# Nine of sixteen x tiles come turned from HBM, and the last products of the second layer come in halves

## The chip, the cores and the metric

The kernel runs on one core of a Trainium2 chip. The core has five engines that run side by side and wait for one another by semaphores: TensorE (PE in the profile; its loads of the stationary operand are PEld), VectorE (DVE), ScalarE (ACT), GpSimd (POOL) and SyncE (SP), which here issues nearly all transfers. The metric is the time of one execution on the device in microseconds, lower is better. The median of three runs before is 492.32 us.

## What is computed

x is 2048 rows of 512 numbers in float32. A layer norm of each row, then two branches on the result, and `x + s * silu(B)` at the end:

```python
xn = (x - mean) / sqrt(var + 1e-5)              # over the 512 columns
q, k, v = split(xn @ wqkv)                      # 32 heads of 16
phi_q = [softmax(q w_phi), softmax(-q w_phi)]   # per head, phi_k alike
s = (phi_q (phi_k^T v)) / (phi_q sum(phi_k) + 1e-6) @ wo
B = mish(xn @ w1 + b1) @ w2                     # 512 -> 1792 -> 512
out = x + s * silu(B)
```

## The kernel before

The 2048 rows are sixteen tiles of 128 rows, t = 0 to 15. Every large product is made of three matmuls: both operands are split into a high part (rounded) and a low part (the rest), and low x high, high x low and high x high are added up in PSUM. ACT makes a high part, DVE or POOL the low part (`split`). The k and v projections, the first layer and one half of the second take seven block products in place of eight, so that sums and differences of two tiles (t and t + 4) are needed as well: `sums_x` makes them (`ts`, split into `th` and `tl`).

`norm(t)` brings a tile to the form in which the products read it, with the 512 columns on the partitions. It loads the tile as x (128 rows on the partitions), takes mean and variance per row on DVE (`bn_stats`, `bn_aggr`), 1/sqrt on POOL (`pow`), normalises the tile on DVE or ACT, turns it with four matmuls against an identity matrix into one PSUM bank `pt`, and splits that bank into the slot `xT`. The bank is read again by `sums_x`, where tile t + 4 is first copied out of PSUM (`xr`), since POOL cannot read there.

Tiles 8 to 15 of the second layer (steps Ga to Gd of the list, `ffn2a` to `ffn2d`) go through the seven products. `ffn2d` is the last: for each of seven blocks b it takes the sum `t4`, split into the slot `md`, and adds its product to the two banks `xb[1][0]` and `xb[1][1]` (x_0 and x_1 below). After the seventh block these banks are the results of output tiles 10 and 11, and `final` (steps E10, E11) applies silu on ACT, multiplies by s and adds x on DVE or POOL, and stores. `PIECES` cuts tile 10 into two and tile 11 into four column pieces there.

Nothing is scheduled by the hardware or by a compiler. The steps in `ORDER` write one long list of operations; `SCHED` is a second list that gives the order in which these are issued, by number, with the engine behind the number where an operation could go to two (V for DVE, G for POOL, A for ACT). `PLACE` gives for each tile the buffer that it lies in. Each engine then takes its own instructions strictly in that order, waiting where an operand or a buffer is not ready. All are issued from one line (L182 before, L185 after), so the profile has to be read by the names of tiles. SP issues the transfers in the same manner; they use eight completion semaphores in turn, so that each transfer also waits for the one eight places ahead of it.

At the start `WAKE` matmuls of ones run on PE while the first loads are on their way, and then eight "folds" (`wkf`, `wqf`: four matmuls each of a weight tile with w_phi).

## Time and profile before

| | before |
|---|---|
| median of three runs | 492.32 us (492.06 to 492.81) |
| profiled execution, its own time | 492.47 us |
| span, first to last instruction | 490.7 us |
| PE busy | 482.5 us, 98% of the span |
| DVE, POOL, ACT busy | 428.0, 276.8, 270.1 us |
| bytes moved | 115.53 MB, 235 GB/s mean |
| granted TensorE clock | 0.996 mean |

A row of a timeline gives the start in us from the span's start, the duration of the group, engine, line, operation, `out<-in`, the size and the count; in square brackets stands how long the engine was idle ahead of it and what ended the wait. A row of the groups view gives `busy us, mean ns of one | idle time before`. A matmul's duration includes its way through the array, and the next one starts before it has ended, so throughput is read from the distance between starts.

### The profile page before, as it was taken

To read this page: it belongs to the slowest core of one execution; us is meant where nothing else is said; L and a number is where in the kernel's file an instruction comes from. 1 tells how busy PE (TensorE), PEld (TensorE's weight loads), DVE (VectorE), ACT (ScalarE), POOL (GpSimd) and SP (SyncE) were. 2 spreads that over 40 slices of the span, in tenths; PEclk is the share of its full clock that TensorE was granted. 3 is DMA by queue.
4 is the path that set the end of the run, shared out by engine and by line. 5 is a ranking of instruction groups with operands and counts; after the bars stand their busy time and mean duration, and the time that the engine had idled before them with its cause. 6 is when DMAs were issued, how large, how long until landed. Compare 5 with 4: busy or idle time off the path is not lost.

```text
span 490.7 us, 8536 instructions
## 1 busy us (share of the span) xinstructions
PE 482.5 (98%) x3126; PEld 397.9 (81%) x3126; DVE 428.0 (87%) x658; ACT 270.1 (55%) x408; POOL 276.8 (56%) x204
## 2 busy tenths in 40 slices
PE   9999999999999999999999999999999999999994
PEld 9888888888888788887888778888888887888883
DVE  5998989999989998989999978979956699889974
ACT  4777754544071524333434778587496487657721
POOL 2889556986548657567575687353642334612440
PEclk9999999999999999999999999999999999999998
DMA  8736838344977689979788896867686652484366
GB/s 296 286 123 243 303 126 338 152 133 120 375 253 265 207 289 342 287 258 298 264 268 286 319 351 233 278 196 234 214 288 230 211 193 67 152 276 154 107 203 203
DMA packets 65592, 115.53 MB, mean 235 GB/s; under 512 B 7056, under 2 KB 32016, under 8 KB 65552
## 3 DMA queue, kind: packets, MB, share of 16 engines
q1 hardware_dynamic: 65408, 114.75, 68.6%
q8 instruction: 24, 0.39, 0.3%
q10 hardware_dynamic: 144, 0.26, 0.1%
q14 instruction: 16, 0.13, 0.1%
HBM read 72.92 MB, written 42.07 MB: 234 GB/s over the span
## 4 chain that ended last, share of the span: by engine, by line
PE 94%; DVE 3%; issue 1%; DMA 1%; POOL 0%; SPq 0%; ACT 0%; DVEq 0%; ACTq 0%
PE y L182 19%; PE fx L182 14%; PE q L182 9%; PE pw L182 9%; PE kx L182 8%; PE fy L182 8%; PE x L182 6%; PE ky L182 4%; PE fz L182 3%; PE pn L182 2%; PE kz L182 2%; PE z L182 2%; PE kvp L182 2%; PE pt L182 1%; PE k L182 1%; PE v L182 1%
## 5 line engine op out<-in xcount | busy, mean ns | idle before, releaser
L182 PE MATMUL q<-wqh,xT 128*128 128x512 f32 x128 | 43.0, 395 | 0.0
L182 ACT ACTIVATE r<-r,b1t 128x512 f32<-128x512 f32 x56 | 37.9, 715 | 3.0 <-DMA r<-hd 3.0
L182 PEld LDWEIGHTS q<-wqh,xT 128*128 128x128 f32 x128 | 24.0, 188 | 5.1
L182 PE MATMUL q<-wql,xT 128*128 128x512 f32 x64 | 25.0, 390 | 0.0
L182 DVE TENSOR_REDUCE tz<-ez 128x64 f32<-128x1024 f32 x16 | 19.3, 1204 | 1.3 <-POOL ez L182 1.3
L182 ACT ACTIVATE hb<-fx 128x512 f32<-128x512 f32 x13 | 7.5, 593 | 18.4 <-PE fx L182 18.4
L182 PE MATMUL kx<-wss,th 128*128 128x512 f32 x56 | 17.3, 390 | 0.0
L182 POOL TENSOR_TENSOR w2t<-w2t 128x256 f32<-128x256 f32 (+1 forms) x4 | 6.0, 1496 | 19.7 <-DVE w2t L182 12.9
L182 ACT ACTIVATE qs<-q 128x512 f32<-128x512 f32 x12 | 6.9, 595 | 17.9 <-PE kvp L182 10.0
L182 POOL TENSOR_TENSOR rs<-rs,mhalf 128x1 f32<-128x1 f32 x16 | 9.8, 620 | 12.0 <-DVE rs L182 11.3
L182 DVE TENSOR_TENSOR ol<-pn,oh 128x256 fp32r<-128x256 f32 x32 | 12.1, 415 | 4.9 <-ACT oh L182 4.9
L182 ACT ACTIVATE hc<-fx 128x512 f32<-128x512 f32 x13 | 7.7, 598 | 15.0 <-PE fx L182 15.0
L182 ACT ACT_TABLE_LOAD x12 | 15.4, 1283 | 0.2
L182 ACT ACTIVATE w1sh<-w1s 128x1024 fp32r<-128x1024 f32 x7 | 7.4, 1059 | 11.8 <-DVE w1s L182 6.2
L182 PEld LDWEIGHTS q<-wql,xT 128*128 128x128 f32 x64 | 12.0, 188 | 2.3
L182 DVE BATCH_NORM_STATS2 st<-x 128x6 f32<-128x512 f32 x16 | 10.7, 682 | 3.6 <-DMA x<-x 3.6
L182 POOL TENSOR_TENSOR w<-w2r,w 128x512 fp32r<-128x512 f32 x7 | 9.0, 1295 | 8.5 <-ACT w L182 8.5
L182 DVE TENSOR_TENSOR xT<-pt,xT 128x512 fp32r<-128x512 f32 x16 | 10.8, 680 | 2.0 <-ACT xT L182 1.2
L182 PE MATMUL pw<-oh,wo0l 128*128 128x512 f32 x32 | 12.5, 390 | 0.0
L182 PE MATMUL pw<-ol,wo0h 128*128 128x512 f32 x32 | 12.5, 389 | 0.0
L182 PE MATMUL pw<-oh,wo0h 128*128 128x512 f32 x32 | 12.5, 389 | 0.0
L182 PE MATMUL pw<-oh,wo1l 128*128 128x512 f32 x32 | 12.4, 389 | 0.0
(862 smaller groups left out, 1864.3 us busy)
## 6 DMA issues: line engine op xcount, KB each, us to landing
r<-hd SPq DMA_DIRECT2D x28, 512.0 KB, 5.3
qd<-qs SPq DMA_DIRECT2D x16, 256.0 KB, 6.3
scr<-xT SPq DMA_DIRECT2D x8, 512.0 KB, 5.3
...
```

What stands on the lines that cost most here:

```text
L182: getattr(g, m)(*a, **k)
```

## The change

Nine tiles (`TURNED`: 3, 6, 7, 9, 10, 11, 13, 14, 15) are no longer turned on PE. The tile is still loaded as x, for the mean and variance. These now stand in the first two columns of a block of 32 columns (`mv`, cleared by POOL first); the reciprocal deviation replaces the variance; DVE turns the block in squares of 32 x 32 (`turn`), so that four of its rows hold the means and four the deviations, 32 numbers or 128 bytes in each. Two transfers write these as two rows of 128 numbers to HBM (`row`), a third reads them back spread over all 128 partitions (`bc`). The tile itself is loaded a second time from `xt`, the transposed copy of x that `final` already uses (`nx`, 512 pieces of 512 bytes). A subtraction and a multiplication of 128 x 512 (DVE or POOL) normalise it, and it lies in SBUF, so that the low part and the sums may go to POOL, and no copy `xr` is needed where tile t + 4 is such a tile.

The last step `ffn2d` becomes three. `ffn2e` splits `t4` (slot `me`) and adds its product to x_0; `ffn2f` and `ffn2g` add to the first and the second half of the columns of x_1, with matmuls of 256 columns. In `ORDER` all of x_0 and its `final` now stand ahead of the second halves.

`WAKE` goes from 13 to 10, and `SCHED` and `PLACE` are new throughout. The first rows of the lists are shown in the diff; what they do is shown by engine below it.

```diff
--- before.py
+++ after.py
@@ -26,9 +26,9 @@
 SLOTS, S2, RQ = 38, 15, 5
-WAKE = 13
+WAKE = 10
 PIECES = {10: 2, 11: 4}
-PLAIN = (0,)
+TURNED = (3, 6, 7, 9, 10, 11, 13, 14, 15)
 GROUPS = ((0, 1, 2, 3), (4, 5, 6))
 ORDER = """
...
-E8 Gc7 O12 Gc8 Gc9 Gc10 Gc11 Gc12 Gc13 Gd7 Gd8 E9 Gd9 Gd10 O10 Gd11 Gd12 E14 E15 E12 E13 Gd13 E10 E11
+E8 Gc7 O12 Gc8 Gc9 Gc10 Gc11 Gc12 Gc13 Ge7 Ge8 E9 Ge9 Ge10 O10 Ge11 Ge12 E14 E15 E12 E13 Ge13 Gf7 Gf8 Gf9 Gf10 Gf11
+Gf12 Gf13 E10 Gg7 Gg8 Gg9 Gg10 Gg11 Gg12 Gg13 E11
 """
 SCHED = """
-27 16 0 13 1 46 2 19 3 15 4 74 5 17 28 6 96 7 14 18 8 123 9 29 10 30 47 20 11 31 12 42 129 48 32 49 33V 50 120 21 51
...
+10 43 0 71 1 12 2 24 238 3 208 93 281 4 13 11 5 14 6 44 15 7 120 45 8 46 72 117 47 9 35 94 48 73 49A 74 25 126 75 36
...
 PLACE = """
-0 2 7 3 1 4 1 6 8 0 3 15 22 2 6 0 0 0 1 7 3 3 9 6 8 4 1 3 1 2 4 10 5 5 13 13 23 30 12 11 14 6 0 5 2 6 7 16 8 4 1 4 7 5
...
+0 0 6 2 17 3 5 7 8 6 12 21 25 3 1 4 5 5 6 9 8 5 10 4 7 1 4 1 3 0 1 18 2 2 11 14 24 30 22 11 15 0 6 2 4 3 4 13 7 7 3 0
...
@@ -324,10 +327,35 @@
         Q.dma_start(xx, x[t * P:(t + 1) * P, :])
         return xx
 
+    def norm_turned(t, mv):
+        rs = mv[:, 1:2]
+        V.tensor_scalar(rs, rs, 1e-5, None, op0=ALU.add)
+        G.tensor_tensor(rs, rs, mhalf, op=ALU.pow)
+        tr = sm([P, 32], f"turn{t}")
+        V.transpose(tr, mv)
+        row = dram.tile([2, P], F32, name=f"row{t}")
+        for c in range(2):
+            Q.dma_start(row[c].rearrange("(b n) -> b n", b=4), tr.rearrange("(b c) n -> c b n", c=32)[c])
+        bc = alloc("s2", [P, 2, P], f"bc{t}")
+        Q.dma_start(bc.rearrange("p c n -> p (c n)"), row.rearrange("c n -> (c n)").partition_broadcast(P))
+        nx = alloc("s2", [P, KC, P], f"nx{t}")
+        Q.dma_start(nx, xt.rearrange("(k p) n -> p k n", p=P)[:, :, t * P:(t + 1) * P])
+        for c, op in ((0, ALU.subtract), (1, ALU.mult)):
+            either(nx, nx, bc[:, None, c, :].to_broadcast([P, KC, P]), op=op)
+        return nx
+
     def norm(t):
         xx = load_x(t)
         st = sm([P, 6], f"st{t}")
         V.bn_stats(st, xx)
+        if t in TURNED:
+            mv = sm([P, 32], f"mv{t}")
+            G.memset(mv, 0.0)
+            V.bn_aggr(mv[:, 0:2], st)
+            w = slot([P, 2, KC, P], f"xT{t}", F32R)
+            pt = norm_turned(t, mv)
+            split(pt, w[:, 0], w[:, 1], either)
+            return keep_x(t, w, pt)
         mv = alloc("st", [P, 2], f"mv{t}")
         V.bn_aggr(mv, st)
         rs = alloc("st", [P, 1], f"rs{t}")
@@ -344,6 +372,9 @@
             for k in range(KC):
                 PE.transpose(pt[:, k, :], xx[:, k * P:(k + 1) * P], ident)
         split(pt, w[:, 0], w[:, 1])
+        keep_x(t, w, pt)
+
+    def keep_x(t, w, pt):
         xT[t], pts[t] = w, pt
         g, i = divmod(t, 4)
         Q.dma_start(scr[g][:, i], f32(w)[:, :, g % 2 * 2:])
@@ -352,18 +383,21 @@
 
     def sums_x(t):
         p1, p2 = pts.pop(t), pts.pop(t + 4)
-        xr = s2(f"xr{t}")
-        copy(xr, p2.rearrange("p k n -> p (k n)"))
-        xr = xr.rearrange("p (k n) -> p k n", k=KC)
+        xr = p2
+        if p2.space == "PSUM":
+            xr = s2(f"xr{t}")
+            copy(xr, p2.rearrange("p k n -> p (k n)"))
+            xr = xr.rearrange("p (k n) -> p k n", k=KC)
+        first = V.tensor_tensor if p1.space == "PSUM" else either
         ts = slot([P, 4, 2, P], f"ts{t}")
-        V.tensor_tensor(ts[:, 0], xr[:, 0:2], p1[:, 0:2], op=ALU.subtract)
+        first(ts[:, 0], xr[:, 0:2], p1[:, 0:2], op=ALU.subtract)
         with one():
             V.tensor_tensor(ts[:, 1], p2[:, 2:4], ts[:, 0], op=ALU.subtract)
             G.tensor_tensor(ts[:, 1], xr[:, 2:4], ts[:, 0], op=ALU.subtract)
         with one():
             V.tensor_tensor(ts[:, 2], p2[:, 2:4], xr[:, 0:2], op=ALU.subtract)
             G.tensor_tensor(ts[:, 2], xr[:, 2:4], xr[:, 0:2], op=ALU.subtract)
-        V.tensor_tensor(ts[:, 3], p1[:, 2:4], ts[:, 1], op=ALU.subtract)
+        first(ts[:, 3], p1[:, 2:4], ts[:, 1], op=ALU.subtract)
         th, tl = (slot([P, 4, 2, P], f"t{n}{t}", F32R) for n in "hl")
         split(ts, th, tl, either)
         tT[t] = th, tl
@@ -605,7 +639,7 @@
             sb["all"] = alloc("tq", [P, 8, 2, 2, 2 * P], "w2sb", F32R)
         sb[b] = split_w2(a[:, 0:2], None, sb["all"][:, b])
 
-    hd, part, sa, sb, t4 = {}, {}, {}, {}, {}
+    hd, part, sa, sb, t4, hd2 = {}, {}, {}, {}, {}, {}
 
     loads, use = [], {}
     for i, bs in enumerate(GROUPS):
@@ -768,6 +802,27 @@
         if last:
             for j in range(2):
                 hs[8 * q + 2 + j] = xb[q][j]
+
+    def ffn2e(n):
+        b = n - NB
+        hl = hd2[b] = slot([P, 2, D], f"me{n}", F32R)
+        split(t4[n], hl[:, 0], hl[:, 1], either)
+        tail(n, 0, 0, D)
+
+    def tail(n, j, c0, c1):
+        b = n - NB
+        wt, hl, c = w2_[b][1], hd2[b], slice(j * P, (j + 1) * P)
+        with one():
+            for m, (u, v) in enumerate(((wt[:, 1, 1, c], hl[:, 0]), (wt[:, 0, 1, c], hl[:, 1]), (wt[:, 0, 1, c], hl[:, 0]))):
+                PE.matmul(xb[1][j][:, c0:c1], u, v[:, c0:c1], start=False, stop=b == NB - 1 and m == 2, skip_group_check=True)
+        if b == NB - 1:
+            hs[10 + j] = xb[1][j]
+
+    def ffn2f(n):
+        tail(n, 1, 0, D // 2)
+
+    def ffn2g(n):
+        tail(n, 1, D // 2, D)
 
     def final(n):
         g, e = divmod(n, 4)
@@ -857,7 +912,7 @@
              "Ka": kv_a, "Kb": kv_b, "Kc": kv_c, "Kd": kv_d, "K": k_plain, "V": v_plain, "A": kv_acc, "Q": q_proj, "S": q_soft, "D": den, "U": num,
              "O": att_out, "L": load_g, "P": prep1, "R": prep2,
              "T": prep2a, "B": prep2b,
-             "Fa": ffn1a, "Fb": ffn1b, "Fc": ffn1c, "Fd": ffn1d, "G": ffn2, "Ga": ffn2a, "Gb": ffn2b, "Gc": ffn2c, "Gd": ffn2d, "E": final}
+             "Fa": ffn1a, "Fb": ffn1b, "Fc": ffn1c, "Fd": ffn1d, "G": ffn2, "Ga": ffn2a, "Gb": ffn2b, "Gc": ffn2c, "Gd": ffn2d, "Ge": ffn2e, "Gf": ffn2f, "Gg": ffn2g, "E": final}
     for c in ORDER.split():
         if c in parts:
             parts[c]()
```

The order of instructions at three places follows, first as it was, then as it is. The numbers in the names are buffers' serial numbers.

The start of the program on PE. `wake` are the matmuls of ones, `wkf` and `wqf` the folds, `pt` the turning of an x tile (x_152 is tile 0, x_164 tile 4, x_180 tile 1), k the first projection. Before:

```order
L182 MATMUL wake<-ones 128x128 x13
L182 MATMUL wkf_163<-phit,wkT_143 128x128 x4
L182 MATMUL wqf_150<-phit,wqT_146 128x128 x4
L182 MATMUL pt_158<-ident,x_152 128x128 x4
L182 MATMUL wkf_162<-phit,wkT_142 128x128 x4
L182 MATMUL pt_170<-ident,x_164 128x128 x4
L182 MATMUL wkf_178<-phit,wkT_144 128x128 x4
L182 MATMUL wqf_197<-phit,wqT_193 128x128 x4
L182 MATMUL wkf_179<-phit,wkT_145 128x128 x4
```

Now:

```order
L185 MATMUL wake<-ones 128x128 x10
L185 MATMUL wkf_162<-phit,wkT_142 128x128 x4
L185 MATMUL pt_170<-ident,x_164 128x128 x4
L185 MATMUL wqf_197<-phit,wqT_193 128x128 x4
L185 MATMUL wkf_163<-phit,wkT_143 128x128 x4
L185 MATMUL pt_158<-ident,x_152 128x128 x4
L185 MATMUL wkf_179<-phit,wkT_145 128x128 x4
L185 MATMUL pt_186<-ident,x_180 128x128 x4
L185 MATMUL wkf_178<-phit,wkT_144 128x128 x4
```

Five folds and three tiles now stand ahead of the first k where six folds and two tiles stood; on SP the loads of x_164 and x_180 have moved ahead of wkT_142, the first fold's weights.

The first turned tile, t = 6, on DVE and on SP. Before, the low part of tile 8 (xT_244) on DVE has short work and one long operation ahead of it:

```order
L182 TENSOR_TENSOR xT_231<-pt_233,xT_231 128x512
L182 BN_STATS st_344<-x_343 128x6
L182 TENSOR_SCALAR nb_281<-mv_278,rs_279 128x1
L182 TENSOR_SCALAR nb_255<-mv_252,rs_253 128x1
L182 TENSOR_TENSOR wv1l<-wvr_211,wv1h 128x1024
L182 TENSOR_TENSOR xT_244<-pt_246,xT_244 128x512
```

Now the subtraction of tile 6 (nx_284, which reads bc_283) stands on DVE three operations ahead of the same low part:

```order
L185 TENSOR_TENSOR wss<-ws_290,wss 128x1024
L185 TENSOR_SCALAR mv_348<-mv_348 128x1
L185 TENSOR_TENSOR nx_284<-nx_284,bc_283 128x512
L185 TENSOR_REDUCE k0s<-k0e 128x64
L185 TENSOR_TENSOR ws_325<-wkr_175,ws_249 128x1024
L185 TENSOR_TENSOR xT_244<-pt_246,xT_244 128x512
```

On SP, the transfers around the same time, as now (row_282 and bc_283 are tile 6, row_303 tile 7, row_266 tile 3; turn_265 is what DVE turned for tile 3):

```order
L185 DMA row_282<-turn_281 4x32
L185 DMA nx_353<-xt 128x4x128
L185 DMA row_303<-turn_302 4x32
L185 DMA nx_268<-xt 128x4x128
L185 DMA scr_102<-xT_156 128x1024
L185 DMA row_282<-turn_281 4x32
L185 DMA qd_109<-qs_275 128x512
L185 DMA row_266<-turn_265 4x32
L185 DMA scrT_106<-tl_174 128x1024
L185 DMA row_303<-turn_302 4x32
L185 DMA bc_283<-row_282 128x256
```

Before, none of these transfers but scr, qd and scrT existed. Tile 6's broadcast is now queued behind the rows of tiles 7 and 3 and behind a store of q.

The end of the program on DVE. h_ are results of other output tiles that still lack a product, u_1119 and u_1116 are tiles 11 and 10 before, u_1123 and u_1120 the same tiles now. Before:

```order
L182 TENSOR_TENSOR h_1071<-h_1071,sr_1110 128x512
L182 TENSOR_TENSOR xx_1109<-h_1071,xx_1109 128x512
L182 TENSOR_TENSOR u_1119<-u_1119,sr_1118 128x128 x3
L182 TENSOR_TENSOR xx_1117<-u_1119,xx_1117 128x128 x3
L182 TENSOR_TENSOR u_1116<-u_1116,sr_1115 128x256 x2
L182 TENSOR_TENSOR xx_1114<-u_1116,xx_1114 128x256 x2
L182 TENSOR_TENSOR u_1119<-u_1119,sr_1118 128x128
L182 TENSOR_TENSOR xx_1117<-u_1119,xx_1117 128x128
```

Now:

```order
L185 TENSOR_TENSOR xx_1111<-h_1076,xx_1111 128x512
L185 TENSOR_TENSOR u_1120<-u_1120,sr_1119 128x256 x2
L185 TENSOR_TENSOR xx_1118<-u_1120,xx_1118 128x256 x2
L185 TENSOR_TENSOR xx_1115<-h_1077,xx_1115 128x512
L185 TENSOR_TENSOR u_1123<-u_1123,sr_1122 128x128 x2
L185 TENSOR_TENSOR xx_1121<-u_1123,xx_1121 128x128 x2
L185 TENSOR_TENSOR u_1123<-u_1123,sr_1122 128x128 x2
L185 TENSOR_TENSOR xx_1121<-u_1123,xx_1121 128x128
```

Tile 10 has moved ahead of a whole tile's last addition, and one of the four pieces of xx_1121 has gone to POOL. On PE the last nine operations are now groups of three matmuls of 256 columns into x_1, where pairs of 512 columns into x_0 and x_1 stood.

156 lines of the change are left out of this document (79 added, 77 removed), and 38 rows, old and new, of the table PLACE.

## The prediction

> **What bounds the kernel now.** I read the page's busy shares and chain first, then what PE waited for, then the timeline of its first microseconds and of the end.
>
> ```profile
> PE 482.5 (98%) x3126; PEld 397.9 (81%) x3126; DVE 428.0 (87%) x658; ACT 270.1 (55%) x408; POOL 276.8 (56%) x204
> PE 94%; DVE 3%; issue 1%; DMA 1%; POOL 0%; SPq 0%; ACT 0%; DVEq 0%; ACTq 0%
> ```
>
> PE is busy 98% of the span and is 94% of the chain that ended last. The whole list of its waits is this:
>
> ```profile
> PE wake L182 <- DVE mhalf L265: 1.1, 1, 1.1
> PE fy L182 <- DVE hc L182: 0.3, 1, 0.3
> PE fy L182 <- DVE ha L182: 0.3, 1, 0.3
> ```
>
> That is 1.1 us before the first instruction and 0.6 us in 480 us of matmuls. The span is therefore PE's own work, plus a start and a tail. Less work on PE shortens it one for one, as long as the other engines follow; each wait that the new list puts on PE lengthens it one for one. The start and one turn of a tile, on PE:
>
> ```profile
> 1.12 5.44 PE L182 MATMUL wake<-ones 128*128 128x128 f32 x26 [1.12 <-DVE mhalf L265]
> 6.39 1.06 PE L182 MATMUL wkf<-phit,wkT 128*128 128x128 f32 x8
> 7.29 1.06 PE L182 MATMUL wqf<-phit,wqT 128*128 128x128 f32 x8
> 8.18 0.60 PE L182 MATMUL pt<-ident,x 128*128 128x128 f32 x4
> 8.62 1.06 PE L182 MATMUL wkf<-phit,wkT 128*128 128x128 f32 x8
> ...
> 12.55 0.47 PE L182 MATMUL k<-wkh,xT 128*128 128x512 f32 x1
> ...
> 20.40 0.60 PE L182 MATMUL pt<-ident,x 128*128 128x128 f32 x4
> 20.75 0.48 PE L182 MATMUL q<-wqh,xT 128*128 128x512 f32 x1
> 21.07 0.39 PE L182 MATMUL q<-wql,xT 128*128 128x512 f32 x1
> 21.30 0.62 PE L182 MATMUL q<-wqh,xT 128*128 128x512 f32 x2
> ```
>
> The starts tell the price. From 21.07 to 21.30 is one matmul of 512 columns, 0.23 us. From the turn at 20.40 to 21.07 are four turning matmuls and one of 512 columns, 0.67 us, so a turn costs 0.44; 8.18 to 8.62 says the same, 0.11 for each of the four. A fold is 8 records in 0.89 us (6.39 to 7.29), 0.11 each. The end, on PE, ACT and DVE in turn:
>
> ```profile
> 482.68 1.52 PE L182 MATMUL x<-md,w 128*128 128x512 f32 x6
> 484.23 1.34 ACT L182 ACTIVATE u<-x 128x128 f32<-128x128 f32 x6 [7.83 <-PE x L182]
> 484.54 0.69 DVE L182 TENSOR_TENSOR u<-u,sr 128x128 f32<-128x128 f32 x3 [2.65 <-DMA out<-xx]
> ...
> 486.43 0.76 DVE L182 TENSOR_TENSOR xx<-u,xx 128x256 f32<-128x256 f32 x2
> 487.10 0.28 DVE L182 TENSOR_TENSOR u<-u,sr 128x128 f32<-128x128 f32 x1
> 487.42 0.29 DVE L182 TENSOR_TENSOR xx<-u,xx 128x128 f32<-128x128 f32 x1
> ```
>
> PE ends at 482.68 + 1.52 = 484.20. Then twelve small operations go through DVE, the last ending at 487.71; what is left to 490.7, 3.0 us, is the last store. So 6.5 us of the span are a tail without PE.
>
> **The change part by part.** The turns: nine tiles of four matmuls leave PE. The row of the group is
>
> ```profile
> L182 PE MATMUL pt<-ident,x 128*128 128x128 f32 x64 | 9.3, 272 | 0.0
> ```
>
> 64 before, 28 now: 36 x 0.11 = **4.0 us less on PE**. Its 272 ns is the way through the array; the distance of starts is the price. I know nothing that excludes all of it; it is lost only where PE comes to wait.
>
> The wake: three of 13 matmuls of ones fewer, 26 records in 5.44 us before, so 0.42 each and 1.26 in all if the first fold could start that much earlier. It cannot, by these rows:
>
> ```profile
> 6.19 0.69 DVE L182 BATCH_NORM_STATS2 st<-x 128x6 f32<-128x512 f32 x1 [0.57 <-DMA x<-x]
> 1.72 0.42 SPq L182 DMA_DIRECT2D x<-x  x1
> ```
>
> x_164 was the second x load issued on an engine's queue and the third large one on any; DVE waited for it until 6.19. Now the weights of the first fold are third on SP, behind two x tiles of the same size, while phic goes on ACT's queue. I take the same for their landing, so the fold starts at about 6.2 in place of 6.39: **0.2 us less**, with 0 and 1.26 as bounds. The wake's other cost is told with the rivals. Between the wake and k stand five folds and three turns, 5 x 0.89 + 3 x 0.44 = 5.8, so k starts at 12.0 or a little later (12.55 before), with one fold more to come later.
>
> The halves of x_1: 21 matmuls of 512 columns become 42 of 256. At a fold's 0.11 a record, with a weight load each, 42 x 0.114 is what 21 x 0.227 was: 0. If each load of weights showed at its full length, 188 ns by this row, it would be 42 x (0.188 - 0.114) = 3.1 us more:
>
> ```profile
> L182 PEld LDWEIGHTS x<-md,w 128*128 128x128 f32 x42 | 7.9, 188 | 1.6
> L182 PEld LDWEIGHTS wkf<-phit,wkT 128*128 128x128 f32 x32 | 3.9, 192 | 0.0
> ```
>
> But a fold's loads last as long, 192, and come every 111 ns; they overlap, so I take 0.
>
> The tail: nine groups of three half-width matmuls stand behind x_0's last, 27 x 0.114 = 3.1 us, in which tile 10's pieces (four DVE operations of 256, 0.38 each by the row at 486.43) pass under PE. Behind the last matmul remain two pieces of tile 11 on ACT (six pieces took 1.34, so about 0.5), then two u and one xx on DVE, 0.3 each: 1.4 us in place of 484.20 to 487.71, 3.5. The store's 3.0 stay. **2.1 us less**, between 0 (if DVE is still at other output tiles) and 2.4. What DVE has to finish in between is seven operations of 512, 7 x 0.61 = 4.3 us, and PE gives it 18 x 0.227 + 33 x 0.114 = 7.8 us from y's last product to the end.
>
> The other engines: over the two lists DVE gets eleven operations of 1024 columns and eight additions of 512 more, and six copies, four normalisations and five head-wise operations of 512 fewer, near 9 us more in all at the rows' 1.2 and 0.68; POOL gets 11 x 2.4 fewer and 10 x 1.3 and 5 x 1.06 more, 8 us less. DVE then stands at 437 of 485 us, 90%. That is no bound on average, but in the stretch of the x tiles there is little left:
>
> ```profile
> 20.00:40.00 20.00, 20.00 (x100) 16.62 (x99) 19.11 (x51) 15.43 (x23) 17.95 (x15) 1.00 0.42 161
> 40.00:60.00 20.00, 20.00 (x98) 16.66 (x97) 18.03 (x41) 14.48 (x22) 14.20 (x12) 1.00 0.68 241
> ```
>
> DVE (the third figure) is busy 19.1 of 20 and 18.0 of 20. The added transfers are nine of 256 KB, nine of 128 KB and eighteen tiny ones: 3.5 of 115.5 MB, in a stretch where the DMA share is 0.42. Their bytes cost nothing; their latency and their places in SP's queue do. The rows for the chain of one turned tile:
>
> ```profile
> 14.14 2.39 POOL L182 TENSOR_TENSOR ws<-wvr,wvr 128x1024 f32<-128x1024 f32 x1
> 20.91 1.06 POOL L182 TENSOR_TENSOR k0e<-kp,k0m 128x512 f32<-128x512 f32 x1
> L182 POOL TENSOR_TENSOR tl<-ts,th 128x1024 fp32r<-128x1024 f32 x5 | 12.0, 2401 | 0.3 <-ACT th L182 0.3
> L182 POOL TENSOR_TENSOR rs<-rs,mhalf 128x1 f32<-128x1 f32 x16 | 9.8, 620 | 12.0 <-DVE rs L182 11.3
> L182 POOL TENSOR_TENSOR mt<-r,r 128x512 f32<-128x512 f32 x3 | 3.9, 1297 | 2.4 <-ACT r L182 2.0 <-PE y L182 0.2
> L182 DVE TENSOR_TENSOR xT<-pt,xT 128x512 fp32r<-128x512 f32 x16 | 10.8, 680 | 2.0 <-ACT xT L182 1.2
> L182 DVE TENSOR_REDUCE tz<-ez 128x64 f32<-128x1024 f32 x16 | 19.3, 1204 | 1.3 <-POOL ez L182 1.3
> L182 ACT ACTIVATE xT<-pt 128x512 fp32r<-128x512 f32 x16 | 9.6, 598 | 5.0 <-PE pt L182 4.5 <-DVE ts L182 0.5
> kvd<-kvf SPq DMA_DIRECT2D x1, 128.0 KB, 3.1
> kvw<-kvd SPq DMA_DIRECT2D x4, 128.0 KB, 5.4
> 6.61 0.47 SPq L182 DMA_DIRECT2D wqT<-wqkT  x1
> ```
>
> For tile 6, the first: POOL has, from the ws at 14.14 to this tile's power, five operations of 1024 (12.0 us), three of about 1 and four powers (2.5): 30 us. SP then waits for tile 3's rows (turn_265), whose power stands two head-wise operations and three powers later: 34. Three transfers on, at 0.47 each, the broadcast is issued at 36. The nearest rows of a small trip through HBM are kvd (written, 3.1 us) and kvw (read back, 5.4); by these it lands between 39.1 and 41.4. DVE subtracts (0.68), POOL multiplies (1.3), ACT makes the high part (0.6), POOL the low (1.3): ready at 45.3 at the latest. PE first reads it after 150 matmuls of 512, three folds and four turns, 34.0 + 2.7 + 1.8 behind k at 12.0: 50.5. Slack 5.
>
> The tight place is behind it on DVE. The subtraction waits there for the broadcast, and three places on comes the low part of tile 8, with 1.2 + 1.2 + 0.68 between: 45.2 by the late landing, 42.9 by the early one. PE wants it 24 matmuls of 512 ahead of tile 6, at 45.1. So the expected wait is about nothing, with no room. A landing of twice 5.4 gives 5.3 us. Other tiles come in later groups with more between. The list before left 0.6 us of waits; for this one, with nine chains of a kind that no row shows, I take **1.0 us more**, bounds 0 and 5.3 for each of three groups.
>
> The sum on the profiled execution: 490.7 - 4.0 - 0.2 - 2.1 + 1.0 = 485.4. Its own time was 492.47, 1.8 outside the span, so **487.2 us**; the median of the runs is 0.15 lower, less than I can tell.
>
> **The rivals.** First, the clock. The wake's records are 0.21 us apart and a fold's 0.11, so the array runs at half pace for nearly all of the wake. Thirteen matmuls lasted long enough for the change of pace; ten end at 1.1 + 10 x 0.42 = 5.3, and PE then rests until 6.2. If the change of pace has not come by then, folds and turns take twice as long until it does: at least the wake's missing 1.3 us at half pace (0.6 lost), at most once more the 5.3 us (2.6 lost). I put 1.5: 488.7. The Trainium skill, "TensorE: Matmul & The Clock Gate", Part 1, says that the array is released after one window of about 3.4 us has been busy, and that the windows run freely; by it the shortened wake would miss in a part of the executions and 1.7 us would be lost then, an estimate from that page. The trace's own change of pace agrees, but shows one execution only.
>
> Second, the gain is eaten. If DVE sets the pace up to 200 us, the 4.0 us off PE are worth nothing there, and the added DVE work of that part, about half of the 9 us, shows: 490.7 - 0.2 - 2.1 + 0 to 4, plus 1.8: about 492, no change. DVE at 93 to 96% in those two rows speaks for it; against it, that POOL, 16 of 20 us busy, is relieved, and that PE never waited for DVE more than 0.3 at once.
>
> Third, slower. The broadcasts land late, SP being held up by a row that waits for DVE, and DVE by a subtraction that waits for SP's broadcast: each holds the other's queue. One landing at twice 5.4 us costs PE 5.3. From two such groups on the change is lost (10.6 against 6.3 gained): 485.4 - 1.0 + 10.6 + 1.8 = 496.8. SP is held up already in the trace before, once for 14.4 us behind a store of q:
>
> ```profile
> SPq L182 <- ACT qs L182: 28.1, 3, 14.4
> ```
>
> That speaks for it; against it speaks that PE has 5 us in hand for the turned tiles themselves. The Trainium skill, "DMA: Bandwidth & Descriptors", Specifications, warns of pieces under 512 bytes, which the 128-byte rows are; it gives no time, no run here shows one, and the bounds above hold without it.
>
> **How the numbers follow.** The forecast 0.56 (485.3 to 489.5, faster), the clock 0.14 (faster), the eaten gain 0.12 (491 to 493, 0.02 of it faster), slower 0.18. With 0.2%, 1 us, as the least that a measurement of this kernel can tell: faster 0.72, no change 0.10, slower 0.18. The range runs from 485.0 (no new waits, the tail at 2.4 and most of the wake's 1.26) to 493.0, leaving out most of the slower case.
>
> **What would show it.** 28 turns on PE and a PE busy time of about 477 to 478; the first fold at 6.2 and at 0.89 us; k at 12 to 12.5; in PE's waits little for xT, th or tl; from PE's end to the span's end 4.4 us. Folds at 1.78 us would be the first rival; DVE waiting for bc and PE for xT of tile 8 the third; many small PE waits for DVE between 30 and 180 us the second. A PE busy time above 481 would mean that the halves are dearer than counted.

## The result and the profile after

The change takes 496.26 us (median of 4, 495.01 to 496.45) against 492.19 for the kernel before run beside it (median of 4, 491.80 to 492.81): a ratio of 1.0076, 95% interval 1.0064 to 1.0089. By that ratio it is slower by 3.7 us (the medians lie 4.1 apart); 487.2 was forecast, faster. The profiled execution took 496.45 us, with a span of 494.7.

The page of the change, its busy times and the shares of its chain by engine:

```profile
PE 482.5 (98%) x3105; PEld 394.5 (80%) x3105; DVE 424.1 (86%) x664; ACT 273.7 (55%) x409; POOL 273.9 (55%) x214
PE 86%; issue 4%; DMA 4%; DVE 3%; ACT 1%; SPq 1%; POOL 0%; POOLq 0%; DVEq 0%; ACTq 0%
```

PE's busy time is to a tenth of a microsecond what it was, although 21 matmuls fewer are issued. Busy time is of no use here: a matmul's modelled end hides a short wait behind it. The chain says more: PE's share has fallen from 94% to 86%, and "issue" and DMA have 4% each. PE's waits, all of them:

```profile
PE fy L185 <- issue: 1.6, 1, 1.6
PE y L185 <- DVE a9l L185: 1.2, 1, 1.2
PE wake L185 <- DVE mhalf L268: 1.1, 1, 1.1
PE pt L185 <- ACT x L185: 0.9, 1, 0.9
PE x L185 <- ACT u L185: 0.7, 2, 0.4
PE pw L185 <- DVE ol L185: 0.7, 1, 0.7
PE fy L185 <- DVE ha L185: 0.5, 1, 0.5
PE pw L185 <- ACT oh L185: 0.3, 1, 0.3
PE wkf L185 <- DMA wkT<-wqkT: 0.3, 1, 0.3
PE z L185 <- DVE ma9l L185: 0.2, 1, 0.2
```

Before, the list was the 1.1 at the wake and twice 0.3. None of the new rows is about a turned tile: no xT, th or tl is waited for.

To see it whole, I counted PE by the distance of starts. Each matmul gets the distance at which its kind runs undisturbed (512 columns 0.227 us, 256 columns 0.113, a turn or fold 0.111, a wake matmul 0.209 for each of its two records, the 1,024 small matmuls kvp and pn 17.8 us together). What the starts need beyond that is time in which PE stood or ran slower.

| us | before | change | difference |
|---|---|---|---|
| matmuls at their undisturbed distance | 479.65 | 474.39 | -5.3 |
| beyond that, between first and last start | 3.27 | 14.41 | +11.1 |
| from the last matmul's start and its own distance to the end of the span, and before the first | 7.8 | 5.9 | -1.9 |
| span | 490.7 | 494.7 | +4.0 |

(The differences are rounded each for itself.)

The 5.3 are 36 turns (4.0) and six wake records (1.25). The work left PE as the prediction said; PE gave back twice as much by standing. Where, worked out from the same starts:

| place | us more than before | what |
|---|---|---|
| to 15 us | 1.4 | the first fold waits for its weights, tile 4's turn for ACT |
| 15 to 145, and 435 on | 1.7 | matmuls that read one tile come 234 ns apart, not 227 |
| 284 | 1.7 | "issue" |
| 418 | 0.4 | DVE late with `ol`, which reads the bank of pn |
| 303 | 1.4 | ACT and, behind it, DVE late for pw |
| 370 to 373 | 1.8 | DVE's low parts a9l and ma9l, beside a multiplication on POOL |
| 488 to 489 | 1.3 | the halves of x_1 |
| all else | 1.3 | half-width matmuls at 120 ns (0.26), waits under 0.3 |

(Rounded each for itself.)

Rows for these. The start, on PE:

```profile
5.37 1.13 PE L185 MATMUL wkf<-phit,wkT 128*128 128x128 f32 x8 [0.29 <-DMA wkT<-wqkT]
7.38 0.66 PE L185 MATMUL pt<-ident,x 128*128 128x128 f32 x4 [0.88 <-ACT x L185]
7.87 1.06 PE L185 MATMUL wqf<-phit,wqT 128*128 128x128 f32 x8
...
12.24 0.47 PE L185 MATMUL k<-wkh,xT 128*128 128x512 f32 x1
```

The stretch around 284 us, on PE, and the last line of the same stretch's transfers that is a piece of some engine's instructions (queue, kind, count, MB, share):

```profile
283.26 0.40 PE L185 MATMUL fy<-ft0h,w1sl 128*128 128x512 f32 x1
283.49 0.40 PE L185 MATMUL fy<-ft0l,w1sh 128*128 128x512 f32 x1
285.45 0.39 PE L185 MATMUL fy<-ft0h,w1sh 128*128 128x512 f32 x1 [1.56 <-issue]
```

```profile
q8 instruction: 1, 0.02, 1.8%
```

Between two matmuls of one group PE stands for 1.73 us beyond its distance, no operand being late: the profile finds no releaser and says "issue". The 0.43 us at 418 are of another kind: the matmul at 418.37 waits for a semaphore of DVE, whose `ol<-pn` ended at 418.22, and in all fourteen kernels with the new list the same time stands ahead of the same matmul. ACT ahead of the waits for pw, held by a transfer:

```profile
300.30 1.34 ACT L185 ACTIVATE r<-r,b1t 128x512 f32<-128x512 f32 x2 [4.52 <-DMA r<-hd]
```

POOL, DVE and PE around 370 us:

```profile
367.69 1.91 DVE L185 TENSOR_TENSOR ma9l<-r,ma9h 128x1024 fp32r<-128x1024 f32 x1 [2.49 <-ACT ma9h L185]
368.48 2.92 POOL L185 TENSOR_TENSOR q14e<-q14e,q14r 128x1024 f32<-128x1024 f32 x1
369.52 2.96 DVE L185 TENSOR_TENSOR a9l<-r,a9h 128x1024 fp32r<-128x1024 f32 x1
372.53 0.50 PE L185 MATMUL y<-a9l,w 128*128 128x512 f32 x1 [1.22 <-DVE a9l L185]
```

The end, on ACT and PE:

```profile
487.80 0.28 ACT L185 ACTIVATE u<-x 128x128 f32<-128x128 f32 x1 [1.49 <-PE x L185]
488.13 0.62 PE L185 MATMUL x<-me,w 128*128 128x256 f32 x3 [0.37 <-ACT u L185]
488.78 0.28 ACT L185 ACTIVATE u<-x 128x128 f32<-128x128 f32 x1 [0.71 <-PE x L185]
489.11 0.97 PE L185 MATMUL x<-me,w 128*128 128x256 f32 x6 [0.37 <-ACT u L185]
```

ACT reads the first half of x_1 (487.80, 488.78) and PE, which writes the other half of the same PSUM tile, waits until it has: 0.64 us lost each time. The prediction has no term for it.

### The profile page after: what moved, and what is told of

Same layout as the page of the kernel before. It is cut to its first block, busy times and chain, and to the rows that moved or that the text cites. A ratio compares the mean times of both kernels' runs of the same rounds, so it can differ in the third digit from the quotient of the medians.

```text
span 494.7 us, 8555 instructions
## 1 busy us (share of the span) xinstructions
PE 482.5 (98%) x3105; PEld 394.5 (80%) x3105; DVE 424.1 (86%) x664; ACT 273.7 (55%) x409; POOL 273.9 (55%) x214
## 4 chain that ended last, share of the span: by engine, by line
PE 86%; issue 4%; DMA 4%; DVE 3%; ACT 1%; SPq 1%; POOL 0%; POOLq 0%; DVEq 0%; ACTq 0%
PE y L185 18%; PE fx L185 14%; PE q L185 9%; PE kx L185 8%; PE pw L185 8%; PE fy L185 7%; PE x L185 6%; PE ky L185 4%; PE fz L185 3%; PE kz L185 2%; DMA r<-hd 2%; PE pn L185 2%; PE z L185 2%; PE kvp L185 2%; DMA hd<-hc 1%
## 5 line engine op out<-in xcount | busy, mean ns | idle before, releaser
L185 ACT ACTIVATE qs<-q 128x512 f32<-128x512 f32 x16 | 9.4, 595 | 21.1 <-PE q L185 11.5
L185 ACT ACTIVATE ha<-fx 128x512 f32<-128x512 f32 x12 | 7.0, 595 | 20.2 <-PE fx L185 10.2
L185 ACT ACTIVATE hc<-fx 128x512 f32<-128x512 f32 x12 | 6.8, 593 | 18.3 <-PE fx L185 7.7
L185 ACT ACTIVATE oh<-pn 128x256 fp32r<-128x256 f32 x32 | 10.3, 391 | 11.3 <-PE pn L185 10.8
L185 ACT ACTIVATE v<-kx 128x512 f32<-128x512 f32 x14 | 8.0, 597 | 13.5 <-PE kx L185 11.4
L185 POOL TENSOR_TENSOR u<-u,sr 128x512 f32<-128x512 f32 x3 | 3.8, 1283 | 20.2 <-DMA sr<-so 13.6
L185 POOL TENSOR_TENSOR w<-w2r,w 128x512 fp32r<-128x512 f32 x9 | 13.8, 1552 | 2.2 <-ACT w L185 2.2
L185 ACT ACTIVATE kp<-kx 128x512 f32<-128x512 f32 x13 | 7.7, 595 | 8.6 <-PE kx L185 5.1
L185 PEld LDWEIGHTS kx<-wss,th 128*128 128x128 f32 x56 | 10.5, 188 | 2.5
```

Source lines behind the costliest of these rows:

```text
L185: getattr(g, m)(*a, **k)
```

## The experiments

Behind each time stand its range and number of runs (n), the ratio to the kernel before as run beside that kernel, and the ratio's 95% interval. A theory A or B in an expectation is one of two rival accounts, each with the time that it would give.

### The address of one tile

The pool of small tiles (`st`) has become shorter, so everything laid out behind it has moved. The tile of tag `tq`, which holds `wss` (the moving operand of 168 matmuls) and later `w2sb` (the weights of 84), began at byte 195328 of a partition, a multiple of 128, and begins at 194464 now, which is 32 past a multiple of 64. Its matmuls are the ones that come 234 ns apart. Two kernels move only this, the change by 32 bytes (to 194496) and the kernel before by 32 bytes (to 195360):

```diff
+    pools["st"].tile([P, 8], F32, tag="stpad", name="stpad")
     places = iter(PLACE.split())
```

> The changed kernel with 32 bytes per partition of padding ahead of the one large tile that holds the split sums of the k and v weights (wss) and later those of w2 (w2sb). The new list gives the pool ahead of it fewer tiles, and so this tile begins at byte 194464, 32 past a multiple of 64; in the kernel before it begins at 195328, a multiple of 64. Nothing else moves. In the profile of the change the 251 matmuls of 512 columns that read it start 233.6 ns apart, all others of that shape 227.5, and in the profile of before all of them 227. Theory A, the address does it: the 251 fall to 227 ns, 1.7 us less, 494.5 us; the other stalls stay. Theory B, something of the neighbourhood does it (transfers, the other engines): the spacing stays at 233 and the time at 496.3.

> The kernel before with the same 32 bytes of padding, so that here the tile leaves the multiple of 64 (byte 195360). Theory A: its 252 matmuls of 512 columns go from 227 to 233.6 ns apart, 1.7 us more, 493.9 us. Theory B: 227 ns and 492.2 us as before.

The kernel before with the pad: 494.10 (493.77 to 495.08, n 5), ratio 1.0034, 1.0022 to 1.0046. Its span grew by 1.6 us, and its two groups came 233.6 and 233.3 ns apart. That is the clean test: one unused tile, and 1.7 us. The change with the pad: 494.87 (n 8), 1.0054, 1.0032 to 1.0075. There the weights came back to 228.9 ns, and the moving operand stayed at 233.4, since 194496 is a multiple of 64 but not of 128. The interval of its ratio overlaps that of the change, so its time alone shows nothing. A third kernel moved the change by 96 bytes to a multiple of 128 (with 13 matmuls of ones, below); both groups then ran at 227. The group of 56 of these matmuls, one row each of before, the change, and the kernel moved by 96 bytes (busy us, mean ns):

```profile
L182 PE MATMUL kx<-wss,th 128*128 128x512 f32 x56 | 17.3, 390 | 0.0
```

```profile
L185 PE MATMUL kx<-wss,th 128*128 128x512 f32 x56 | 17.6, 396 | 0.0
```

```profile
L185 PE MATMUL kx<-wss,th 128*128 128x512 f32 x56 | 17.3, 389 | 0.0
```

The 7 ns show in the mean length too, at 396 against 390 and 389.

### The chain of the turned tiles

To see whether the round trip through HBM costs anything, the rows and the broadcasts are taken out and a tile of ones stands in their place, so this kernel leaves out the normalisation of the nine tiles.

```diff
-            Q.dma_start(row[c].rearrange("(b n) -> b n", b=4), tr.rearrange("(b c) n -> c b n", c=32)[c])
+            prog.ops.append({"Q": []})
...
-        Q.dma_start(bc.rearrange("p c n -> p (c n)"), row.rearrange("c n -> (c n)").partition_broadcast(P))
+        prog.ops.append({"Q": []})
...
-            either(nx, nx, bc[:, None, c, :].to_broadcast([P, KC, P]), op=op)
+            either(nx, nx, ones[:, None, :].to_broadcast([P, KC, P]), op=op)
```

> The changed kernel without the eighteen row stores and the nine broadcast loads; the nine tiles are subtracted from and multiplied by a constant tile of ones instead of the mean and the deviation, so the normalisation of these tiles is left out, and everything else is issued as it is. Theory A, the loss lies at single places of the new list and at the address, not at the turned tiles: 496.0 us, between 495.3 and 496.8, and the stalls at 7.4, 285.5, 303 to 304 and 370 to 373 us are there again. Theory B, the loss comes from the small trips through HBM, which hold SP's queue (7.1 us of waits for a row) and delay all that is issued behind them: 493 us or less, with those stalls smaller.

495.59 (494.29 to 496.19, n 4), 1.0058, 1.0044 to 1.0072, against 1.0076 with the chain; the intervals overlap. The same edit on a mended kernel (below) gave 491.04 against 491.22. No cost of the rows and broadcasts can be told in either, and the third rival falls. Its rows in the change, SP's issue of tile 6's second row and of its broadcast, then DVE's subtraction that waits for it, and the low part of tile 8:

```profile
31.86 0.51 SPq L185 DMA_DIRECT2D row<-turn  x1
...
35.57 0.32 SPq L185 DMA_DIRECT2D bc<-row  x1
```

```profile
39.86 0.69 DVE L185 TENSOR_TENSOR nx<-nx,bc 128x512 f32<-128x512 f32 x1 [0.47 <-DMA bc<-row]
...
42.93 0.68 DVE L185 TENSOR_TENSOR xT<-pt,xT 128x512 fp32r<-128x512 f32 x1
```

### The clock at the start, and "issue"

The first rival blames ten matmuls of ones in place of 13. So the change gets 13 again, and a second kernel has the 96 bytes as well:

```diff
-    for _ in range(WAKE):
-        PE.matmul(wake, ones, ones, start=True, stop=True)
+    for i in range(WAKE):
+        with one():
+            for _ in range(4 if i == WAKE - 1 else 1):
+                PE.matmul(wake, ones, ones, start=True, stop=True)
```

> The changed kernel with thirteen matmuls of ones at its start in place of ten, nothing else. In the four profiles of kernels with ten, the records were 0.21 us apart (half pace) until 4.1, 6.0, 10.1 and 10.5 us, in the two with thirteen until 6.0 and 4.7. Where it lasted to 10, a fold took 1.7 us in place of 0.89 and the first product with k started at 13.9 and 14.6 us in place of 12.2. Theory A, the shortened wake ends before the change of pace in part of the executions: with thirteen the folds take 0.89 us, k starts at 12.3 to 12.8 us, the runs lie within 1.5 us of one another, and the median is 0.5 to 1.5 us less, 495.3 us. Theory B, the wake does not matter because the first fold waits for its weights in any case (until 5.4 to 7.4 us): 496.3 us, with k as late as before.

> Thirteen matmuls of ones, and 96 bytes of padding, so that the tile of wss and w2sb begins at byte 194560, a multiple of 128 (and 256). With 32 bytes of padding (a multiple of 64, not of 128) the 84 matmuls that load w2sb as weights fell from 233.3 to 228.9 ns, while the 167 that stream wss stayed at 233.4. Theory A, a tile read as the moving operand has to begin at a multiple of 128 bytes: both at 227 ns, 1.7 us less than with thirteen matmuls of ones alone, about 493.6 us. Theory B, only the weights' side was the address and the rest is the neighbourhood: wss stays at 233, and the time is 0.4 us less.

Thirteen made it worse: 498.95 (497.43 to 499.83, n 4), 1.013, 1.0112 to 1.0147; with the address put right 494.25 (n 8), 1.0046, 1.0028 to 1.0064. That is 4.7 us less for 96 bytes where 1.7 was expected; the other 3 are open. The start was as intended, but something far behind it had moved. The first of the two, PE at 285 us, and three stretches from there on (their limits, length, PE, PEld, DVE, ACT, POOL busy, clock, DMA share, GB/s):

```profile
280.64 1.80 PE L185 MATMUL pn<-ph,kvw 32*32 32x256 f32 x74
285.64 0.58 PE L185 MATMUL pn<-ph,kvw 32*32 32x256 f32 x1 [3.20 <-issue]
```

```profile
282.00:285.60 3.60, 0.44 (x26) 0.00 (x0) 1.02 (x2) 2.82 (x7) 3.60 (x4) 0.97 0.64 246
285.60:292.40 6.80, 6.76 (x16) 4.92 (x16) 1.74 (x4) 1.22 (x3) 5.27 (x3) 0.51 0.24 75
292.40:300.00 7.60, 7.60 (x151) 5.57 (x150) 5.95 (x14) 2.60 (x8) 5.07 (x3) 1.00 0.84 243
```

The "issue" wait grew from 1.73 to 3.55 us and now lies among the small pn matmuls, a little earlier in the program. Behind it the clock is at half for 6.8 us. Three matmuls more on PE at the start, which are twelve instructions (two records and two weight loads each), changed a wait at 284 us.

What ties the two is how PE gets its instructions. The instruction queue q8 has 24 transfers of 16 KB in the change, and PE has 6280 records in the trace (3105 matmuls, as many weight loads, 70 others, mostly waits for semaphores); 6280 / 256 is 24.5, so one piece is about 256 of them. Counted so, this wait stands behind the same number of records, 3777, in all six kernels that have it (the change, the one with 32 bytes, the one without broadcasts, the one with loads moved below, and the two with 13 ones), whichever matmul comes there. PE ran through the 256 records ahead of it in 3.71 us in the change (1.73 us of wait) and in 2.68 with 13 ones (3.55). With boundaries every 256 records from there, the fastest piece of the kernel before took 5.39 us, and none ended in such a wait. (The expectations below count the pieces' times from undisturbed distances and put some boundaries elsewhere; they took the 0.43 us at 418 for such a wait.) The transfer in the row above comes at 283.04, as PE nears the end of the piece; the one before it came at 248.71, and PE goes on at 285.45, 2.4 us behind the later one. The Trainium skill, "Runtime: NRT & Kernel Launch", Instruction fetch mechanics, says that instructions come in blocks of 16 KiB, 256 of them, and that the cost of a boundary is mostly hidden. The count agrees; here it was not hidden. No row names the wait for what it is, so the test is to move the boundaries. First the change with 13 ones, 96 bytes and 32 tiny matmuls, then the kernel before with the tiny ones alone, then the change with 17 tiny ones alone:

```diff
+            for _ in range(32 if i == WAKE - 1 else 0):
+                PE.matmul(wake[0:1, 0:1], ones[:, 0:1], ones[:, 0:1], start=True, stop=True)
```

> As the one with thirteen matmuls of ones and 96 bytes of padding, and 32 further matmuls of one column by one column behind the wake: some 128 records more on PE (64 loads, 64 matmuls), which move every boundary between two 16 KB pieces of PE's instructions by about half a piece; no transfer of data is moved. With the two loads moved, PE's stall at 285 us went from 1.73 to 0.82 us, but the transfer of instructions came no earlier relative to the block of 256 small instructions (pn) ahead of the stall: 0.6 us behind its end before, at its end then. Theory A, two boundaries lie at the two ends of that block (records 3507 and 3762 of about 255 each, at 279.2 and 282.1 us) and PE runs through a whole piece in 2.7 us, faster than the next comes: with the boundary in the middle of the block the stall is under 0.4 us, and the time 1.3 us less than without the 32, about 492.3 us. Theory B, the data on the DMA engines delays the piece: the stall stays at 1.5 to 1.8 us, and the time the same or up to 0.5 us more.

> The kernel before with 32 more matmuls of one column by one column behind the wake, 128 records, so that every boundary between two 16 KB pieces of PE's instructions (one per 256 records, the known ones at records 1985 and 3776) lies 128 records earlier in the work. The fastest of all pieces then takes 1.9 us, twice (in the second block of kvp at 133 us and the third at 175 us), and a third takes 3.1 us (pn at 406); in the kernel before as it is none takes under 5.1 us. The 32 themselves cost 0.4 us at the start. Theory A, a piece that PE works off in less time than the next takes to come (3.6 us and less stood still so far, 3.8 for 0.4 us, 4.1 and more not) makes PE stand: stalls of 1.5 to 3.5 us at 135 to 137 and at 176 to 178 us and one of about 1 us at 410, half pace behind one of them in part of the executions, 496 to 500 us, widely spread. Theory B, such stalls belong to the transfers of the changed kernel: none here, 492.8 us.

> The changed kernel with 17 such matmuls of one column behind the wake (68 records) and nothing else. By the same count its fastest piece then takes 3.8 us (pn at 403 us), the next 4.8, where without them one takes 3.6 at 274 to 278 us. Theory A: the stall of 1.7 us at 285 is gone, the half pace that follows it in part of the executions too; the 0.4 us at 418 stays; 2 us less, 494.2 us. Theory B, the order of the transfers makes it: the stall stays, 496.5 us.

The first: 494.59 (n 12), 1.0041, 1.0023 to 1.006. The wait at 285 us was gone, and one of 1.9 us stood at 137.5, among the kvp matmuls. The time is not below the 494.25 without the tiny ones, where 1.3 us less was expected; the runs lie between 491.98 and 496.34, and the profiled one, 492.24, is one of the fastest. The kernel before: 499.28 (498.87 to 499.87, n 4), 1.014, 1.0127 to 1.0154. Two waits that it never had came among the kvp matmuls, at two boundaries whose pieces now took 1.8 us each: 3.15 us until 140.93 and 1.88 until 184.9:

```profile
137.47 0.51 PE L182 MATMUL kvp<-k8e,v 128*32 128x64 f32 x22
140.93 0.33 PE L182 MATMUL kvp<-k8e,v 128*32 128x64 f32 x9 [2.94 <-issue]
```

Of its 7 us, 5.0 are these and 2.1 are at the start, where the tiny ones ran at half pace, k coming at 14.71; 0.4 was expected for them. A third piece, which ends at 418.7 us, took 2.68 us, as long as the one that ended in 3.55 with 13 ones, and no wait came there: how fast is too fast is not a fixed number. No half pace followed the 3.15 us; with 13 ones and 96 bytes it did follow a wait of 3.48. The two stretches behind these waits, the latter first (the clock is the third figure from the end):

```profile
284.20:289.60 5.40, 5.40 (x13) 3.85 (x13) 1.02 (x2) 1.27 (x3) 4.50 (x2) 0.50 0.09 31
140.90:148.00 7.10, 7.08 (x70) 5.91 (x70) 5.96 (x8) 2.65 (x5) 2.32 (x1) 1.00 0.32 102
```

Two counts over the traces say more than any one wait. The boundaries at which PE stood are three, behind 1985, 2753 and 3777 records to within one, and these differ by 768 and 1024, 3 and 4 times 256, in the kernel before as in the change. And in all nine waits, in eight kernels, PE went on 2.3 to 2.5 us after a transfer on q8 had begun.

The change with 17: 493.12 (491.56 to 496.74, n 12), 1.0019, 1.0002 to 1.0036, and no "issue" row in its list. So with 17 tiny matmuls, 68 instructions that do nothing, the change took some 3 us less. Between the two profiles (2.3 us) the wait is 1.7 of it; the waits for pw, which come and go, are 1.2 less as well, and other waits are longer.

The rival itself was tried from the other side, the kernel before with ten ones:

```diff
-WAKE = 13
+WAKE = 10
...
+    prog.ops += [{"PE": []}] * 3
```

> The kernel before with ten matmuls of ones in place of thirteen, nothing else. Theory A: the half pace lasts beyond the wake in part of the executions; the runs spread over 2 us or more (1.1 us with thirteen: 491.95 to 493.08), and the median is 0.3 to 1.5 us more than before, 493.2 us. Theory B: same time or up to 0.3 us less, 492.2 us, with no wider spread.

491.94 (n 11), 0.9992, 0.9983 to 1.0001: no difference. For the "issue" wait I had first suspected two large loads that fall due beside it, and moved them 33 and 56 places back in the list:

```diff
-... 1251 1482 1289G 1204 1188 1212 1191 1219 1528 1228A ... 1230 1290 ... 1253 1642 ...
+... 1251 1289G 1204 1188 1212 1191 1219 1228A ... 1230 1482 1290 ... 1253 1528 1642 ...
```

> The changed kernel with two loads on SP's queue moved later: the 512 KB of r for tile 2 of the third group (issued at 275.8 us) and the 256 KB of xx for tile 2 (277.6 us) now stand behind the store of hc at 286.6 us. In the profile PE stands from 283.7 to 285.45 us in the middle of a product, with its weights loaded and no semaphore to wait for. A 16 KB transfer of the queue that carries PE's instructions (one per 255 of PE's records in quiet stretches) is due by that count at 277.6 us and comes at 283.04, at the end of seven microseconds in which the DMA engines are full; 256 small matmuls and loads fall into that time. Theory A, PE ran out of instructions because their transfer stood behind data: with 0.77 MB, about 2 us, less ahead of it the stall is gone or under 0.5 us, and the kernel takes about 1.6 us less, 494.6 us. Theory B, PE stood because of ACT, whose table load runs from 284.07 to 285.36 us just then: the stall stays, 496.3 us.

493.24 (491.46 to 495.87, n 12), 1.0015, 0.9999 to 1.0031. In its profile 0.82 us of the wait stayed: with less traffic around it the piece came sooner, but the wait did not go. The median fell by 3 us where 1.6 was expected, as much as with 17 tiny matmuls, and the profiled execution (495.26) is one of the slowest of its twelve; so the traffic counts beside the boundary, and how much each is worth in the median is open. This kernel's profile also shows the clock rival at work, since its fold began late:

```profile
6.30 2.04 PE L185 MATMUL wkf<-phit,wkT 128*128 128x128 f32 x8 [0.56 <-DMA wkT<-wqkT]
8.14 1.06 PE L185 MATMUL pt<-ident,x 128*128 128x128 f32 x4
9.00 1.56 PE L185 MATMUL wqf<-phit,wqT 128*128 128x128 f32 x8
10.39 1.06 PE L185 MATMUL wkf<-phit,wkT 128*128 128x128 f32 x8
...
13.87 0.48 PE L185 MATMUL k<-wkh,xT 128*128 128x512 f32 x1
```

The first fold takes twice its time, and the pace changes at 10.06 only; k is at 13.87 in place of 12.24. From the first fold to k it takes 7.56 us, where five folds and three turns at full pace take 5.8, so 1.8 are lost. Of four profiles of the change's start, two changed pace early (4.05 and 6.03) and two late (10.5 and 10.06), the first fold starting at 5.37 and 5.83 in the former, 7.39 and 6.31 in the latter (there 1.4 and 1.8 us were lost).

### The change mended

Now 13 ones, 96 bytes, and 14 tiny matmuls, 68 instructions in all again, by which the fastest piece ends in no wait:

> The changed kernel with thirteen matmuls of ones, 96 bytes of padding and 14 matmuls of one column (the fastest piece 3.8 us, the next 4.8). Theory A, what was lost beside the list were the address (1.7 us), the pieces (1.7, and 4 more where half pace follows) and the late change of pace at the start (up to 2): all three go, stalls remain at 160 (0.6), at 303 (0.3 to 1.4), at 370 to 373 (1.4) and in the tail (1.3). From the profile with thirteen and 96 bytes, 497.1 us, of which 6.6 between 275 and 295 us: 490.9 us, within 1.5 us of one another. Theory B, the new list itself loses the time by its order: 493.5 us or more.

491.22 (490.77 to 492.56, n 12), 0.9977, 0.9966 to 0.9987. The same without the broadcasts, and the same with ten ones and 17 tiny ones:

> The mended change (thirteen matmuls of ones, 96 bytes, 14 of one column) without the eighteen row stores and nine broadcast loads; the nine tiles are normalised by a constant tile of ones, so their normalisation is left out. Theory A, the trips through HBM cost PE nothing: 491.2 us as with them, within 0.5. Theory B, they hold SP and DVE up and the rest of the list pays: 1 us or more less, 490.2 or under.

> The mended change with ten matmuls of ones and 17 of one column in place of thirteen and 14, so that the pieces lie where they did. Theory A, the wake that ends before the weights of the first fold have come leaves PE idle, and the change of pace is missed in part of the executions: the median is 0.3 to 1.5 us above that with thirteen (491.2), and the runs spread over 2.5 us or more (1.8 with thirteen). Theory B, the small matmuls and the fold keep PE busy long enough and the wake is of no weight: 491.0 us, same spread.

491.04 (n 8), 0.9974, 0.9962 to 0.9985; 491.37 (n 12), 0.9982, 0.9969 to 0.9994. Neither the chain nor three matmuls of ones can be told from nothing in the median. But the last is no test of the rival, since its tiny matmuls fill the time up to the first fold (the last starts at 6.25 us, the fold at 6.34); in the kernel before with ten the fold came at 5.54, right behind the wake too. Against the kernel with 17 tiny ones and the old address (493.12) the last is 1.75 lower: the address once more.

The waits of the list come next. Three edits together: the late r's on ACT behind the last oh, a9l and ma9l exchanged on DVE, x_1's pieces directly behind the halves:

```diff
-1395 1404 (ahead of 1281)      1525V ... 1565V   1527 ... 1568
+1281 1395 1404                 1565V ... 1525V   1568 ... 1527
...
+1940 1964 1960 1954            (x_1's pieces)
```

> The same with three edits of the list: two Mish operations of ACT on rows 0_1 and 0_2, which wait for their load at 296 to 300 us, behind the four copies that pw waits for; DVE's low part a9l ahead of ma9l, and PE's products with a9 (six matmuls) ahead of those with ma9; in the tail the two pieces of ACT on the first half of x_1 directly behind its last matmul, so that PE waits once instead of twice. Theory A: no stall at 303, under 0.3 us at 370 to 373, one of 0.6 us in place of two of 0.64 in the tail: 2 us less than without these edits, 488.9 us. Theory B, time gained at one of these places is lost at the next, since DVE and ACT are as late there: under 0.7 us less.

492.11 (490.98 to 493.86, n 12), 0.9995, 0.9984 to 1.0006, not better; 488.9 was expected under theory A. The exchange moved the wait from a9l to ma9l (0.36 + 1.39 us on PE), and a new one for a1l of 0.84 came at 316.8. So the order of the two is not the matter. Their length is: next to q14e on POOL (2.92 us, where five of the eight others of its kind on POOL took 1.94) the subtraction took 2.96, where others took 1.22. The next kernel puts that one multiplication on DVE:

```diff
-1427G
+1427V
```

> The mended change with one multiplication, that of q14e by q14r at 365 us, on DVE in place of POOL. In all six profiles looked at, the one of DVE's subtractions of 1024 columns that meets it takes 2.3 to 2.96 us where others take 1.22, and it takes 2.92 itself where others on POOL take 1.94; PE waits 1.4 us for the subtraction. Theory A, the two engines hold each other up while both read and write these tiles: both subtractions take 1.2 to 1.3 us, PE's waits at 366 to 369 (0.8 and 1.4 in the profile) fall under 0.3, 1.8 us less, 489.4 us. Theory B, DVE's subtraction is late for another reason, or the 1.2 us that DVE now has to do itself come back at the next place: 490.8 to 491.5 us.

490.07 (489.69 to 491.06, n 5), 0.9957, 0.9945 to 0.9969: faster than both kernels, and between the times of the two theories. POOL and DVE there, and all of PE's waits that its list shows:

```profile
363.00 1.29 POOL L185 TENSOR_TENSOR u<-u,sr 128x512 f32<-128x512 f32 x1 [13.45 <-DMA sr<-so]
363.58 1.80 DVE L185 TENSOR_TENSOR ma9l<-r,ma9h 128x1024 fp32r<-128x1024 f32 x1 [2.49 <-ACT ma9h L185]
365.30 1.21 DVE L185 TENSOR_TENSOR a9l<-r,a9h 128x1024 fp32r<-128x1024 f32 x1
366.43 1.21 DVE L185 TENSOR_TENSOR ez<-q15e,zb 128x1024 f32<-128x1024 f32 x1
367.56 1.21 DVE L185 TENSOR_TENSOR q14e<-q14e,q14r 128x1024 f32<-128x1024 f32 x1
```

```profile
PE wake L185 <- DVE mhalf L269: 1.1, 1, 1.1
PE x L185 <- ACT u L185: 0.7, 2, 0.4
PE fy L185 <- DVE ha L185: 0.5, 1, 0.5
```

DVE now does a9l and q14e in 1.21 us each, where the subtraction alone took 2.96 beside POOL; ma9l, which still meets POOL's u, still takes 1.80. PE's standing at these two places fell from 2.2 us to 0.3. The ends fit one engine waiting for the other: in the change a9l ends at 372.48, 1.08 behind the end of POOL's q14e (371.40), and here ma9l ends at 365.38, 1.09 behind POOL's u (364.29). The Trainium skill, "SBUF — State Buffer", SBUF: two separate sides, says that VectorE with two inputs in SBUF and GpSimd hold a shared pair of ports exclusively, one waiting for the whole operation of the other; these ends, and 2.92 and 2.96 against 1.94 and 1.22, agree with it.

> The same as the last, and in the tail ACT's first two pieces of x_1 directly behind the last matmul of its first half. In the profiles PE waits twice 0.64 us in the tail for ACT to have read a part of x_1 that PE no longer writes; with this order it waited once, 0.70. Theory A: 0.5 us less than without, 488.9 us. Theory B, the end is set by the last pieces behind PE and not by PE: the same as without.

This has the pieces of x_1 directly behind the halves as well: 490.35 (489.77 to 491.47, n 5), 0.996, 0.9948 to 0.9972. One of the two waits at the end went (0.70 left in place of 1.28), and the time cannot be told from the one above.

## Why the prediction was wrong

The step that failed is the term "1.0 us more" for new waits: it measured 11.1. It was looked for in one place, the chain of the turned tiles, and there it was nothing; each piece of it lay elsewhere. For two of the causes, the address of one tile and the boundaries between pieces of PE's instructions, the sum had no term at all.

- **The turns.** Right: 28 are left, and 4.0 us left PE, by the starts.
- **The wake and the start.** Forecast 0.2 less, measured 0.2 more (1.25 of wake against 1.4 of standing). The fold began at 5.37, not 6.2: the landing taken from x_164 was too late for this execution, and within 5.37 to 7.39 over four. That tile 4's turn would wait 0.9 us for ACT was not counted. k came at 12.24 as forecast here, at 12.1 to 14.6 over four.
- **The halves of x_1.** The price of a half, 0.120 us in place of 0.114, was about right (0.26 in all). What was missed is that the two halves share a PSUM tile with ACT's reads: 1.28.
- **The tail.** 1.9 us less from PE's end to the span's end, forecast 2.1.
- **The chain.** Right in each time, in one of them by luck: the terms from 14.14 to tile 6's power add up to 31.6, not 30, and it came out because POOL began that work at 12.30. The broadcast was issued at 35.57 (forecast 36), and DVE subtracted at 39.86, after 0.5 us of waiting (a landing between 39.1 and 41.4 was forecast). Tile 6 was ready at 44.75 (45.3), first read at 51.16 (50.5). Tile 8's low part, the tight place, ended at 43.61, and PE wanted it at 45.71 (45.1). (A landing of twice 5.4 would by the same terms have cost 5.5, not 5.3.)
- **The other engines.** DVE was busy 424.1 us where 437 was forecast, POOL 273.9 where some 269 was. The counts of operations were right, the durations not: on DVE others became shorter (sixteen of 128 x 32 took 3.3 us in place of 6.5), and on POOL the fifteen further operations of 512 columns went with 25.6 us more where 18.3 was counted.
- **The rivals.** The clock came in two of four profiles and cost 1.8 and 1.4 us up to k there, near the 1.5 put on it; in the profiled execution of the change, from which the 11.1 is read, the pace changed in time. No kernel tests it in the changed list by itself (13 ones also moved a boundary), so its share in the change's median is open. The eaten gain did not come, and DVE's two rows were misread for it: they say 96% and 90%, not 93 to 96. The third put its time at 496.8, near the 496.26 measured, by luck: its mechanism is one that the chain's rows and two kernels without the broadcasts refute.
- **What would show it.** "A PE busy time above 481 would mean that the halves are dearer" was a wrong sign: 482.5 came from waits, which busy time hides, and from the address.

The 11.1 is shown in parts: the address by the kernel before with a pad (1.7), the boundaries of the instruction pieces by adding idle instructions to either kernel (1.7 in the profile, near 3 in the medians, of which traffic and other waits may be a part), POOL beside DVE by moving one operation (about 1 of the 1.8). The 0.4 at 418, the end (1.3) and the start (1.4) are read from rows, and the end was mended only in part, with no gain that could be measured. The 1.4 at 303 us is open. Behind ACT's r, which waits 4.52 us for hd from HBM, the two waits for pw came in some executions (0.96 in the change's, 1.77 with 32 bytes) and not in others (none in the first mended one), with the list unchanged. Open also is why half pace followed waits of 3.55 and 3.48 us in two kernels and did not follow 3.15 in a third; these are a single execution each.
